# Four early loads on a second queue, and two MoE blocks summed chunk by chunk, in an attention + MoE kernel with a planned order

## The chip, the cores and the metric

The kernel runs on one core of one Trainium2 chip. The metric is the device time of one execution in microseconds (us). Engines are called TensorE (matmuls; PE in the profile), VectorE (DVE), ScalarE (ACT), GpSimd (POOL) and SyncE (SP). SyncE issues the loads and stores; 16 DMA engines move the bytes.

## The reference, cut to what matters

```python
# q, k, v: (4, 8, 768, 64) float32; w_in (512, 2048), w_out (2048, 512) float64
k_sum = k.reshape(B, H, 24, 32, D).max(axis=3)      # block maxima of the keys
v_sum = v.reshape(B, H, 24, 32, D).mean(axis=3)     # block means of the values
scores_l = scale * q @ k.T                          # kept where |i - j| < 16
scores_s = scale * q @ k_sum.T + log(32)
a = softmax(concat([masked scores_l, scores_s]))
x = (a @ concat([v, v_sum])).reshape(3072, 512)     # tokens x (heads * 64)
h = x @ w_in
out = (h - tanh(h)) @ w_out
```

## The kernel before, in words

The 3072 tokens are handled in 8 units of 384 (half a sequence of one batch). Of each unit, attention is computed for four pairs of heads: queries and keys are transposed on TensorE (`prep`), scores are made for three tiles of 128 tokens (`scores`), VectorE and ScalarE do the softmax, the probabilities are transposed, and `values` multiplies them with a value tile `vw`, whose rows hold a window of values and the 24 block means. `x_split` evicts a pair's result (for unit 0 as plain float32 into a tile `xh`, one of four slices per pair). Then the MoE runs in 16 blocks of 128 hidden columns: `moe_in` (four chunks of 128 rows, one per head pair, summed in a PSUM bank `pH`), an activation on ScalarE and VectorE (tiles `gt`, `gu`, `gh`), and `moe_out` into three banks `pY`.

The weights come as float64. 32 loads of 512 KB (weight 2f is block f's part of w_in, weight 2f+1 its part of w_out) go through three places of one buffer, `raw` (weight i uses place i % 3), and `convert` makes float32 of each by bit operations: a scale copy on ScalarE (or VectorE) into `qa` or `tmp`, and on VectorE the low bits (`w low`), the sign (`w sign`; both in place in `raw`) and the join into `wf`. After its first use in unit 0 each weight is split into a high and a low part (`split_whole`) for the later units, which use three faster matmuls instead of one exact one.

The block means of the first batch come from two loads of 768 KB (`first_means(0, g)`, tile `xh`), added pairwise and summed on TensorE with a matrix `blk`; `put_mean` copies them into `vw`.

Nothing is written in the order in which it runs. Every step is a task with a cost per engine; `Plan.schedule` walks through time, and gives the engine that can start first its startable task with the greatest level (the longest path behind it, plus entries of the tables `BIAS` and `KB`; `SL` says when a task may go to a second engine). The resulting order is then emitted, and each engine runs its own instructions strictly in that order, waiting for what they need. In the plan, transfers follow one another on one line, a SyncE task is not started when more than 3 us of transfers (`QUEUE`) or eight loads (`LANES`) are ahead of it, and TensorE's gaps before 100 us (`WARM`) are filled with matmuls of the identity into the bank `pX` (`keep_warm`), whose results nobody uses. The plan has a model of TensorE's clock (`Clock`).

On the chip SyncE's queue issues a load when its buffer is free and the earlier loads have been issued. All instructions are recorded under one line of a helper (L67), so that tiles and not lines tell them apart: `xl` is the first batch's keys, `rawq` queries, `vw` value tiles, `vsum` the value means of the second batch, `chunk` and `vacc` those of the later ones, `k` and `q` the transposed operands, `probw` and `stat` the softmax, `wh` and `wl` the split weights.

Of the kernel before, what the change touches and what calls it, by code (L numbers as in the profile page):

```python
# [12 lines left out]
U32 = mybir.dt.uint32  # L13
# [45 lines left out]
class Engine:  # L59


    def __init__(self, tc, engine):
        self._tc, self._engine = tc, engine

    def __getattr__(self, name):
        op = getattr(self._engine, name)
        return lambda *args, **kwargs: self._tc.keep_in_program_order(op(*args, **kwargs))  # L67


class Task:  # L70
    __slots__ = ("index", "costs", "go", "after", "order", "level", "count", "ready", "next", "start", "engine", "cost", "place", "out", "banks", "behind", "moves", "kind", "name")
# [28 lines left out]
class Plan:  # L100

    SEEN = {PE: 0.2, ACT: 0.16, DVE: 0.13, POOL: 0.1, SP: 0.95}
    ISSUE = 0.5
    QUEUE = 3.0  # L110
    AHEAD = 1.1
    LANES = 8

    def __init__(self):
        self.tasks, self.rings, self.place, self.banks, self.count = [], {}, {}, set(), {}
        self.writer, self.readers, self.touch, self.first = {}, {}, {}, {}

# [7 lines left out]
    def add(self, kind, costs, go, r=(), w=(), before=()):  # L125
        t = Task()
        t.index, t.kind, t.costs, t.go = len(self.tasks), kind, costs, go
# [13 lines left out]
        for base in {key[0] for key in (*r, *w)}:  # L141
# [20 lines left out]
    def schedule(self, idle):  # L162
# [18 lines left out]
        dma, held = 0.0, {DVE: 0.0, POOL: 0.0}  # L181
# [121 lines left out]
def program(  # L303
# [14 lines left out]
    P = 128  # L318
# [831 lines left out]
```

## Time and profile before

| | us |
|---|---|
| median of 3 runs | 740.21 (739.56 to 740.95) |
| the profiled execution | 741.52 |
| its span, first to last instruction | 740.0 |
| TensorE busy | 711.1 (96%) |
| VectorE busy | 508.6 (69%) |
| ScalarE busy | 461.0 (62%) |
| GpSimd busy | 148.0 (20%) |
| mean granted clock of TensorE | 0.988 |
| bytes moved, all by SyncE's queue but for 0.9 MB of instructions | 53.97 MB |

Busy times are sums of records; a busy TensorE is not one at its peak, because matmuls are pipelined. The granted clock is a share of 2.4 GHz; the lower of its two levels, 1.2 GHz, shows as 0.5.

### The profile page before, as it was taken

How to read it: one execution, taken by the hardware profiler on the slowest of the kernel's cores; microseconds unless marked ns; L12 is line 12 of the kernel's file. 1: busy time of each engine (PE TensorE's matmuls, PEld its weight loads, DVE VectorE, ACT ScalarE, POOL GpSimd, SP SyncE). 2: the span in 40 equal slices, each digit the busy share in tenths (PEclk: the TensorE clock that was granted, in tenths of full speed). 3: DMA queues.
4: the chain of work that ended last, by engine and by line, in shares of the span. 5: the costliest groups of instructions: out<-in, count | busy, mean ns of one | idle time of the engine just before them, and what ended most of it. 6: DMA issues, size and time to landing. Idle time of an engine off the chain costs nothing.

```text
span 740.0 us, 13051 instructions
## 1 busy us (share of the span) xinstructions
PE 711.1 (96%) x4205; PEld 589.0 (80%) x4205; DVE 508.6 (69%) x1788; ACT 461.0 (62%) x1388; POOL 148.0 (20%) x229
## 2 busy tenths in 40 slices
PE   7888988999999999999999999999999999999995
PEld 5554444558888888989988889889988899889993
DVE  3789999678876689577765786677665557753332
ACT  2677775557876576667675776766565666754230
POOL 5131000012331013224231133212232132110000
PEclk9899999999999999999999999999999999999998
DMA  9886666602020322422020341212020201101001
GB/s 215 211 221 201 198 200 227 117 2 64 1 63 1 84 85 58 90 51 77 1 63 1 83 108 37 47 35 70 1 62 1 54 30 23 40 2 43 1 0 49
DMA packets 109510, 53.97 MB, mean 73 GB/s; under 512 B 90808, under 2 KB 102776, under 8 KB 109432
## 3 DMA queue, kind: packets, MB, share of 16 engines
q1 hardware_dynamic: 109432, 53.03, 27.5%
q8 instruction: 36, 0.59, 0.3%
q14 instruction: 42, 0.34, 0.2%
HBM read 44.95 MB, written 6.29 MB: 69 GB/s over the span
## 4 chain that ended last, share of the span: by engine, by line
PE 80%; DVE 10%; DMA 3%; SPq 2%; ACT 2%; issue 1%; POOL 1%; DVEq 0%; ACTq 0%
PE pY L67 33%; PE pH L67 33%; PE pS L67 6%; PE pT L67 4%; PE pX L67 3%; DVE raw L67 3%; DVE wf L67 3%; SPq L67 2%; DMA raw<-in_moe_w_in_dram 1%; DVE probw L67 1%; DMA raw<-in_moe_w_out_dram 1%; DMA vw<-in_v_dram 1%; DVE vacc L67 1%; DVE gh L67 0%; DVE stat L67 0%
## 5 line engine op out<-in xcount | busy, mean ns | idle before, releaser
L67 PE MATMUL pH<-xh,wf 128*128 128x384 f32 x548 | 188.0, 377 | 5.0 <-ACT gt L67 3.2
L67 PE MATMUL pY<-wf,gh 128*128 128x512 f32 x432 | 177.8, 438 | 0.5 <-DVE gh L67 0.5
L67 ACT ACTIVATE gu<-pH 128x384 f32<-128x384 f32 x128 | 62.6, 489 | 131.7 <-PE pH L67 124.5
L67 PEld LDWEIGHTS pH<-xh,wf 128*128 128x128 f32 x548 | 103.2, 190 | 26.9 <-ACT gt L67 4.4
L67 POOL TENSOR_TENSOR gl<-gv,gh 128x384 fp32r<-128x384 f32 x57 | 58.5, 1027 | 243.6 <-ACT gh L67 117.2
L67 PEld LDWEIGHTS pY<-wf,gh 128*128 128x128 f32 x432 | 80.6, 190 | 22.3 <-issue 11.2
L67 DVE CUSTOM_DVE_ANT_0 prob<-pS,mask 64x118 f32<-64x118 f32 x288 | 80.2, 278 | 24.6 <-PE pT L67 9.1
L67 PE MATMUL pH<-xh,wh 128*128 128x384 f32 x252 | 88.2, 350 | 0.0
L67 PE MATMUL pH<-xl,wh 128*128 128x384 f32 x252 | 85.0, 337 | 0.0
L67 ACT ACTIVATE prob<-prob,stat 128x118 f32<-128x118 f32 x175 | 67.8, 392 | 26.6 <-DVE stat L67 22.4
L67 PE MATMUL pY<-wh,gh 128*128 128x512 f32 x168 | 70.9, 422 | 0.0
L67 ACT ACTIVATE gu<-gu 128x384 f32<-128x384 f32 x128 | 66.8, 523 | 0.0
L67 PE MATMUL pY<-wh,gl 128*128 128x512 f32 x168 | 66.3, 394 | 0.0
L67 DVE CAST gh<-gv 128x384 fp32r<-128x384 f32 x59 | 21.2, 359 | 59.9 <-PE pY L67 59.6
L67 ACT ACTIVATE gt<-pH 128x384 f32<-128x384 f32 x128 | 61.7, 482 | 0.0
L67 DVE TENSOR_TENSOR gv<-gu,gt 128x384 f32<-128x384 f32 x68 | 38.9, 572 | 20.5 <-ACT gu L67 13.4
L67 POOL TENSOR_TENSOR gv<-gu,gt 128x384 f32<-128x384 f32 x44 | 45.3, 1029 | 34.6 <-DVE gl L67 16.1
L67 PEld LDWEIGHTS pH<-xh,wh 128*128 128x128 f32 x252 | 47.4, 188 | 2.2 <-issue 0.5
L67 PE MATMUL pS<-k,q 128*128 128x364 f32 (+1 forms) x176 | 44.9, 336 | 3.3 <-DVE stat L67 2.7
L67 PEld LDWEIGHTS pH<-xl,wh 128*128 128x128 f32 x252 | 47.3, 188 | 0.0
L67 ACT ACTIVATE probT<-pT 118x256 f32<-118x256 f32 x86 | 32.6, 379 | 20.9 <-PE pT L67 20.8
L67 PEld LDWEIGHTS pS<-k,q 128*128 128x128 f32 x176 | 30.7, 190 | 13.1 <-issue 5.1
(185 smaller groups left out, 1484.1 us busy)
## 6 DMA issues: line engine op xcount, KB each, us to landing
raw<-in_moe_w_in_dram SPq DMA_DIRECT2D x16, 512.0 KB
raw<-in_moe_w_out_dram SPq DMA_DIRECT2D x16, 512.0 KB
rawq<-in_q_dram SPq DMA_DIRECT2D x48, 128.0 KB
out_dram<-tmp SPq DMA_DIRECT2D x23, 256.0 KB
raw<-in_k_dram SPq DMA_DIRECT2D x24, 192.0 KB
vw<-in_v_dram SPq DMA_DIRECT2D x40, 96.0 KB
vw<-in_v_dram SPq DMA_DIRECT2D x48, 64.0 KB
chunk<-in_v_dram SPq DMA_DIRECT2D x16, 192.0 KB
```

The costliest lines, as they stand in the source:

```text
L67: return lambda *args, **kwargs: self._tc.keep_in_program_order(op(*args, **kwargs))
```

## The change

- `convert`: the loads of weights 0 and 2 are issued by ScalarE instead of SyncE. `first_means(0, g)`: so are the two 768 KB loads of the first batch. All other loads stay with SyncE. In the plan such a load takes 0.5 us (`ISSUE`) of ScalarE's time and its bytes join the one line of transfers; it is not held back by `QUEUE` or `LANES`.
- `Plan.schedule`: before 60 us, a SyncE load whose transfer is costed at over 1.25 us and that follows a smaller one is planned to hold the line for 0.9 us more.
- `moe_in`: in unit 0, blocks 0 and 1 become four tasks each, one per chunk, of 0.68 us, instead of one of 2.65. The matmuls are the same ones.
- The tables: `BIAS` 763 entries instead of 539 (360 as before), `SL` 44 instead of 43 (7 as before), `KB` 158 instead of 156 (44 as before).

```diff
...
+    LARGE, TURN = 1.25, 0.9
...
             t.start, t.engine, t.cost = now, e, t.costs[e]
+            if t.moved is not None:
+
+                t.moves = max(dma, now + self.AHEAD)
+                dma = t.moves + t.moved
...
             if e == SP:
                 free[e] = now + self.ISSUE
                 t.moves = max(dma, now + self.AHEAD)
-                dma = t.moves + t.cost
+                dma = t.moves + t.cost + (self.TURN if t.cost > self.LARGE and not large and now < 60.0 else 0.0)
+                large = t.cost > self.LARGE
                 landed.append(dma + self.SEEN[e])
                 release(t, dma + self.SEEN[e])
             else:
                 free[e] = clock.run(now, t.cost) if e == PE else now + t.cost
-                release(t, free[e] + self.SEEN[e])
+                release(t, free[e] + self.SEEN[e] if t.moved is None else dma + self.SEEN[SP])
...
-    def dma(kind, go, nbytes, run, r=(), w=(), before=()):
+    def dma(kind, go, nbytes, run, r=(), w=(), before=(), by=SP):
         rate = 227e3 if run < 512 else 302e3 if run < 1024 else 356e3 if run < 4096 else 390e3
-        do(kind, SP, nbytes / rate, go, r, w, before)
+        if by is not SP:
+            plan.add(kind, {by: plan.ISSUE}, lambda: go(engines[by]), r, w, before, nbytes / rate)
+            return
+        do(kind, SP, nbytes / rate, lambda: go(sync), r, w, before)
...
-        dma("w load", load, P * 8 * DM, 1024 if i % 2 == 0 else 4096, w=RAW)
+        dma("w load", load, P * 8 * DM, 1024 if i % 2 == 0 else 4096, w=RAW, by=ACT if i in (0, 2) else SP)
...
-        dma("v load", lambda: sync.dma_start(at(base), v[b, HG * g:HG * (g + 1)].rearrange("h (r t) d -> r h (t d)", t=6)), S * HG * D * 4, 1536, w=[(base, 0)])
+        dma("v load", lambda e: e.dma_start(at(base), v[b, HG * g:HG * (g + 1)].rearrange("h (r t) d -> r h (t d)", t=6)), S * HG * D * 4, 1536, w=[(base, 0)], by=SP if b else ACT)
...
         if u == 0:
-            def go():
+            def go(cs):
+                for c in cs:
+                    tensor.matmul(at(ph)[:, :U], at(("wf", i))[:, P * c:P * (c + 1)], at(xf)[:, c], start=c == 0, stop=c == NC - 1)
+            if f < 2:
+
                 for c in range(NC):
-                    tensor.matmul(at(ph)[:, :U], at(("wf", i))[:, P * c:P * (c + 1)], at(xf)[:, c], start=c == 0, stop=c == NC - 1)
-            do("in", PE, 2.65, go, r=[(("wf", i), 0)] + [(xf, c) for c in range(NC)], w=[(ph, 0)])
+                    do("in" if c == NC - 1 else "in part", PE, 0.68, lambda c=c: go([c]), r=[(("wf", i), 0), (xf, c)], w=[(ph, 0)])
+            else:
+                do("in", PE, 2.65, lambda: go(range(NC)), r=[(("wf", i), 0)] + [(xf, c) for c in range(NC)], w=[(ph, 0)])
             split_whole(i)
             return
```

## Rows read from the trace of the kernel before

**Rows 1.** Busy us (instructions) of each engine by stretches; then clock, DMA share, GB/s.
```profile
0.00:12.00 12.00, 7.99 (x46) 6.93 (x47) 1.30 (x7) 1.99 (x3) 8.31 (x34) 1.00 0.82 194
12.00:26.00 14.00, 11.11 (x62) 7.13 (x60) 12.59 (x55) 9.54 (x38) 3.84 (x10) 1.00 1.09 241
26.00:33.00 7.00, 6.31 (x32) 4.81 (x32) 3.61 (x17) 1.95 (x5) 0.21 (x1) 0.54 0.61 148
33.00:50.00 17.00, 13.99 (x135) 9.36 (x134) 15.59 (x58) 14.98 (x50) 4.85 (x12) 0.99 0.88 230
...
60.00:128.00 68.00, 61.87 (x242) 33.34 (x242) 66.36 (x174) 48.18 (x129) 4.35 (x8) 1.00 0.64 206
...
140.00:731.00 591.00, 589.89 (x3636) 517.52 (x3634) 393.87 (x1444) 370.85 (x1132) 124.33 (x163) 1.00 0.17 41
...
sum 740.00, PE 711.06 PEld 588.95 DVE 508.58 ACT 460.96 POOL 148.01; mean PE 79.01 PEld 65.44 DVE 56.51 ACT 51.22 POOL 16.45
```

**Rows 2.** Timeline, VectorE and ScalarE: start, us, what, [idle before <-releaser].
```profile
8.66 0.96 DVE L67 TENSOR_TENSOR xh<-xh 128x768 f32<-128x768 f32 x1 [7.33 <-DMA xh<-in_v_dram]
...
11.19 0.37 ACT L67 ACTIVATE mean<-pT 24x256 f32<-24x256 f32 x1 [9.11 <-PE pT L67]
```

**Rows 3.** Timeline, TensorE, near 26 us.
```profile
26.66 1.41 PE L67 MATMUL pX<-probT,vw 118*64 118x64 f32 x16 [2.34 <-DMA vw<-in_v_dram]
```

**Rows 4.** Chain of waits from 60 to 145 us, shares by line.
```profile
by line: DVE raw L67 24.1%; DVE wf L67 20.0%; DMA raw<-in_moe_w_in_dram 11.9%; PE pH L67 8.4%; DVE probw L67 6.7%; PE pY L67 6.3%; issue 5.1%; DVE vacc L67 4.0%; PE pT L67 3.6%; DVE gh L67 3.0%; DVE stat L67 1.0%; DVE tmp L67 0.9%; PE pX L6
```

**Rows 5.** SyncE's waits from 0 to 140 us: total us, times, longest.
```profile
SPq L67 <- DVE wf L67: 27.2, 15, 3.7
```

**Rows 6.** Timeline of SyncE's queue: the four loads, and weight 3.
```profile
1.88 0.54 SPq L67 DMA_DIRECT2D xh<-in_v_dram  x1
...
10.28 0.78 SPq L67 DMA_DIRECT2D xh<-in_v_dram  x1
...
17.16 0.43 SPq L67 DMA_DIRECT2D raw<-in_moe_w_in_dram  x1
...
19.22 0.43 SPq L67 DMA_DIRECT2D raw<-in_moe_w_in_dram  x1
...
45.06 0.35 SPq L67 DMA_DIRECT2D raw<-in_moe_w_out_dram  x1
```

**Rows 7.** Groups of conversion instructions, 0 to 140 us: busy us, mean ns.
```profile
L67 DVE TENSOR_SCALAR raw<-raw 128x512 uint16<-128x512 uint16 x32 | 23.2, 746 | 0.1
...
L67 DVE SCALAR_TENSOR_TENSOR wf<-tmp,raw 128x512 uint32<-128x512 uint32 x21 | 14.4, 692 | 0.1
L67 DVE TENSOR_SCALAR raw<-raw 128x512 uint32<-128x512 uint32 x32 | 13.5, 426 | 3.4 <-DMA raw<-in_moe_w_out_dram 2.8 <-DMA raw<-in_moe_w_in_dram 0.6
...
L67 ACT ACTIVATE tmp<-raw 128x512 f32<-128x512 f32 x16 | 10.6, 677 | 7.9 <-DMA raw<-in_moe_w_in_dram 6.4 <-DMA raw<-in_moe_w_out_dram 1.0
```

**Rows 8.** Timeline, VectorE and ScalarE, 36 to 53 us: evictions of pairs, conversion.
```profile
36.22 0.48 ACT L67 ACTIVATE xh<-pX 128x384 f32<-128x384 f32 x1
...
36.95 0.75 DVE L67 TENSOR_SCALAR raw<-raw 128x512 uint32<-128x512 uint32 x2
...
43.88 0.47 ACT L67 ACTIVATE xh<-pX 128x384 f32<-128x384 f32 x1
...
44.27 0.72 DVE L67 SCALAR_TENSOR_TENSOR wf<-qa,raw 128x512 uint32<-128x512 uint32 x1
...
46.03 0.69 DVE L67 SCALAR_TENSOR_TENSOR wf<-tmp,raw 128x512 uint32<-128x512 uint32 x1
...
52.55 0.43 DVE L67 TENSOR_SCALAR raw<-raw 128x512 uint32<-128x512 uint32 x1 [2.63 <-DMA raw<-in_moe_w_out_dram]
```

**Rows 9.** Timeline, TensorE: first query transposes; warm-up and first MoE blocks.
```profile
11.08 0.55 PE L67 MATMUL pH<-ident,rawq 128*128 128x128 f32 x3
...
49.24 0.49 PE L67 MATMUL pX<-ident 128*128 128x128 f32 x2
49.56 5.33 PE L67 MATMUL pH<-xh,wf 128*128 128x384 f32 x16
```

More of the change, by code (lines that the diff above doesn't have):

```diff
@@ new lines @@
+SL = {('w scale', 0, 'vector'): 1, ('k again', 2, 'gpsimd'): 0.6, ('normal', 0, 'scalar'): 0.6, ('q high', 2, 'vector'): -0.6, ('top low', 1, 'gpsimd'): 1, ('normal', 2, 'scalar'): 1, ('k again', 2, 'scalar'): 1.5, ('k high', 0, 'vector'): 0.6, ('top low', 2, 'gpsimd'): -0.6, ('p out', 0, 'vector'): 1, ('g high', 2, 'vector'): 0.6, ('w scale', 1, 'vector'): 4, ('sum guard', 2, 'gpsimd'): 0.3, ('p out', 1, 'vector'): -0.6, ('g high', 1, 'vector'): -0.3, ('x whole', 2, 'vector'): -0.6, ('x high', 2, 'vector'): -0.3, ('k again', 1, 'gpsimd'): 0.6, ('w high part 2', 0, 'vector'): 0, ('top put', 2, 'vector'): 0, ('q again', 2, 'scalar'): 0, ('q again', 1, 'gpsimd'): 0.6, ('top put', 0, 'vector'): 4, ('k again', 1, 'scalar'): 2.5, ('top put', 2, 'scalar'): 0.3, ('p out', 2, 'vector'): 1.5, ('normal', 1, 'scalar'): -0.6, ('top high', 1, 'scalar'): -0.3, ('g', 2, 'vector'): 1.5, ('top put', 1, 'scalar'): 2.5, ('k high', 2, 'vector'): 2.5, ('x high', 0, 'vector'): -0.6, ('x high', 1, 'vector'): 0.6, ('q again', 2, 'gpsimd'): -0.3, ('sum guard', 1, 'gpsimd'): 4, ('pair', 2, 'vector'): 0, ('q again', 1, 'scalar'): 1, ('top put', 1, 'vector'): 2.5, ('q high', 1, 'vector'): 0.6, ('q high', 0, 'vector'): 0.6, ('k high', 1, 'vector'): -0.6, ('g low', 1, 'vector'): 2.5, ('w high part 2', 1, 'vector'): 0.3, ('top high', 2, 'scalar'): -0.6}
@@ new lines @@
+KB = {('square', 1): 220, ('exp', 2): 102, ('out', 2): -19, ('values', 1): 28, ('w scale', 1): 112, ('k turn', 2): -38, ('g high', 2): -96, ('k low', 1): -494, ('g high', 1): -340, ('top put', 2): 151, ('pick', 2): 18, ('w low part', 1): 63, ('series', 2): 64, ('top put', 0): 109, ('square', 2): 57, ('mean turn', 1): -73, ('w low', 1): -57, ('w load', 1): -48, ('w low', 0): 97, ('x high', 0): 38, ('exp', 0): 28, ('series', 1): 130, ('p turn', 2): -50, ('inverse', 2): 137, ('x high', 2): 37, ('values', 2): 2, ('w high part', 1): 19, ('out', 1): -11, ('q low', 1): -459, ('big', 1): -123, ('tanh', 1): -169, ('direct', 1): 24, ('scores', 2): 6, ('in', 2): -93, ('normal', 2): -41, ('mean out', 0): -57, ('min', 2): -53, ('mean out', 1): 102, ('cube', 2): -140, ('exp', 1): -111, ('mean turn', 0): 122, ('in', 0): -13, ('q high', 0): 6, ('top max', 0): -64, ('top low', 0): -194, ('g low', 2): 18, ('k high', 1): -58, ('k turn', 0): 23, ('w shift', 0): -153, ('top turn', 0): 15, ('p out', 2): 11, ('sum out', 0): -33, ('k high', 0): 16, ('min', 0): 42, ('big', 2): 18, ('sum guard', 0): 7, ('sum', 0): 28, ('w load', 0): 56, ('q turn', 0): 56, ('values', 0): 30, ('w high part', 0): 111, ('k load', 0): 191, ('v load', 0): -38, ('p out', 0): 11, ('min', 1): 82, ('normal', 0): 75, ('sum guard', 1): -293, ('x high', 1): 186, ('q high', 1): -43, ('inverse', 1): -61, ('g low', 1): 12, ('p turn', 0): 18, ('k turn', 1): 37, ('top pre', 0): 17, ('square', 0): 82, ('pick', 1): -55, ('p out', 1): 61, ('in', 1): 21, ('p turn', 1): -31, ('pick', 0): 21, ('direct', 0): -139, ('cube', 0): 30, ('w sign', 1): -216, ('g', 1): -48, ('cube', 1): -7, ('big', 0): 97, ('w sign 2', 0): 34, ('q turn', 1): 21, ('normal', 1): -28, ('w sign 2', 1): 17, ('q again', 1): -53, ('mean put', 1): 101, ('w high part 2', 1): -123, ('g', 0): 84, ('g', 2): 15, ('x low', 0): -1, ('seen max', 2): 2000, ('w shift', 1): -15, ('y store', 2): 148, ('chunk load', 0): 8, ('top put', 1): -188, ('k high', 2): -195, ('k again', 2): -113, ('tanh', 0): -67, ('top turn', 2): -3, ('x low', 1): -89, ('w sign', 0): 90, ('w scale', 0): -57, ('chunk load', 2): 3, ('x whole', 2): -89, ('w high part 2', 0): 272, ('w low part 2', 2): 70, ('top high', 2): 21, ('chunk sum', 2): 79, ('k load', 1): 7, ('mean turn', 2): -121, ('w high part 2', 2): 144, ('k low', 2): 125, ('k again', 1): -307, ('top low', 1): -114, ('top low', 2): -166, ('mean put', 0): 21, ('out', 0): -61, ('q load', 2): -92, ('inverse', 0): 9, ('top high', 1): -20, ('tanh', 2): 61, ('seen', 2): 2000, ('series', 0): -26, ('k load', 2): 92, ('q high', 2): -100, ('scores', 1): 24, ('q again', 2): 9, ('pad', 2): -162, ('w low part 2', 1): 115, ('const', 0): -168, ('chunk sum', 0): -2, ('q load', 1): -74, ('x low', 2): 12, ('q load', 0): -2, ('v load', 1): 20, ('mean put', 2): 43, ('top max', 1): -65, ('seen turn', 2): 2000, ('w sign', 2): -130, ('top turn', 1): 15, ('mean out', 2): -226, ('mean copy', 0): 145, ('y out', 2): 61, ('w join', 2): 107, ('sum guard', 2): -22, ('w join', 0): -32, ('q low', 2): -78, ('q turn', 2): 8, ('w join', 1): -71, ('v load', 2): -87, ('pair', 2): 30, ('in part', 2): -11}
@@ L70 @@
 class Task:
-    __slots__ = ("index", "costs", "go", "after", "order", "level", "count", "ready", "next", "start", "engine", "cost", "place", "out", "banks", "behind", "moves", "kind", "name")
+    __slots__ = ("index", "costs", "go", "after", "order", "level", "count", "ready", "next", "start", "engine", "cost", "place", "out", "banks", "behind", "moves", "moved", "kind", "name")
 HELD = {"pair", "mean copy", "w join", "w shift", "w low", "w sign", "w low part", "w low part 2", "w low part 3", "w high part", "w high part 2", "w scale", "normal", "g high", "g low", "g", "cube", "big", "k again", "q again", "top pre", "sum guard"}
@@ L123, in users, with add @@
         return {t for key in keys for t in (self.writer[key], *self.readers.get(key, ()))}
-    def add(self, kind, costs, go, r=(), w=(), before=()):
+    def add(self, kind, costs, go, r=(), w=(), before=(), moved=None):
         t = Task()
+        t.moved = moved
         t.index, t.kind, t.costs, t.go = len(self.tasks), kind, costs, go
@@ L180, in schedule @@
         landed = [0.0] * self.LANES
-        dma, held = 0.0, {DVE: 0.0, POOL: 0.0}
+        dma, large, held = 0.0, False, {DVE: 0.0, POOL: 0.0}
         clock = Clock()
@@ L599, in load_k @@
         for h in range(HG):
-            dma("k load", lambda h=h: sync.dma_start(tile()[:, :, h], k[b, HG * g + h].rearrange("(c r) d -> r c d", c=6)), S * D * 4, D * 4, w=[keys[h]], before=before)
+            dma("k load", lambda e, h=h: e.dma_start(tile()[:, :, h], k[b, HG * g + h].rearrange("(c r) d -> r c d", c=6)), S * D * 4, D * 4, w=[keys[h]], before=before)
     def first_means(b, g, tag):
@@ L625, in sum_chunks @@
             dr = v[b, HG * g:HG * (g + 1)].rearrange("h (n t) d -> (h n) t d", t=32)
-            dma("chunk load", lambda st=st, dr=dr, c=c: sync.dma_start(at(st)[:96], dr[:, 8 * c:8 * c + 8, :]), 96 * 2048, 2048, w=[(st, 0)])
+            dma("chunk load", lambda e, st=st, dr=dr, c=c: e.dma_start(at(st)[:96], dr[:, 8 * c:8 * c + 8, :]), 96 * 2048, 2048, w=[(st, 0)])
             def total(c=c, st=st):
@@ L647, in load_q @@
         for i in range(NT):
-            dma("q load", lambda i=i: sync.dma_start(at(rawq)[:, i], qd[b, t0 + P * i:t0 + P * (i + 1), HG * g:HG * (g + 1), :]), P * HG * D * 4, D * 4, w=[(rawq, i)])
+            dma("q load", lambda e, i=i: e.dma_start(at(rawq)[:, i], qd[b, t0 + P * i:t0 + P * (i + 1), HG * g:HG * (g + 1), :]), P * HG * D * 4, D * 4, w=[(rawq, i)])
     def load_v(u, g):
@@ L656, in rows @@
             s0 = t0 + off + P * i
-            dma("v load", lambda: sync.dma_start(at(vw)[r0:r1, i, half], vd[b, s0:s0 + r1 - r0, hs, :]), (r1 - r0) * HG * D * 4, D * 4, w=[vw_keys(vw, i, half)[m] for m in parts])
+            dma("v load", lambda e: e.dma_start(at(vw)[r0:r1, i, half], vd[b, s0:s0 + r1 - r0, hs, :]), (r1 - r0) * HG * D * 4, D * 4, w=[vw_keys(vw, i, half)[m] for m in parts])
         for i in range(NT):
             if u % 2 == 0 and i == 0:
-                dma("v load", lambda: sync.dma_start(at(vw)[0:WIN + 1, 0, 0], vd[b, 0:1, hs, :].broadcast_to([WIN + 1, HG, D])), (WIN + 1) * HG * D * 4, D * 4, w=[vw_keys(vw, 0, 0)[0]])
+                dma("v load", lambda e: e.dma_start(at(vw)[0:WIN + 1, 0, 0], vd[b, 0:1, hs, :].broadcast_to([WIN + 1, HG, D])), (WIN + 1) * HG * D * 4, D * 4, w=[vw_keys(vw, 0, 0)[0]])
                 rows(0, [0], WIN + 1, 64, WIN + 1, 0)
@@ L684, in put_mean @@
             else:
-                dma("mean put", lambda to=to, x=x: sync.dma_start(to(), x), NT * NB * HG * D * 4, 1024, r=[MEAN[g]], w=keys)
+                dma("mean put", lambda e, to=to, x=x: e.dma_start(to(), x), NT * NB * HG * D * 4, 1024, r=[MEAN[g]], w=keys)
     def operands(u, p):
@@ L1018, in store_y @@
         r = u * U + P * i
-        dma("y store", lambda: sync.dma_start(out[r:r + P, :], at(ys)), P * DM * 4, 2048, r=[(ys, 0)])
+        dma("y store", lambda e: e.dma_start(out[r:r + P, :], at(ys)), P * DM * 4, 2048, r=[(ys, 0)])
     NS = NP * SLOTS * NU
```

10 lines of the change are left out of this document (4 added, 6 removed).

## The prediction

> **What bounds the kernel now.** I read three views: the busy time by stretches of the span, then the chain of waits in the stretch that is not full of matmuls, then SyncE's own waits. In the first the reader is to see where TensorE is not busy: over the whole span it is busy for 711.06 of 740 us, and from 140 to 731 us for 589.89 of 591, at full clock [rows 1]. I take that part, and the last 9 us (last tile out, last check), as fixed. What can move lies in the first 140 us, in three regimes:
> - 0 to 26 us: the transfers. The DMA share is 0.82 and then 1.09 (records overlap, so over 1 is possible), and VectorE is idle for 10.7 of the first 12 us, 7.33 of them in one wait for the first value tile [rows 1, 2].
> - 26 to 60 us: mixed. From 26 to 33 us TensorE has a granted clock of 0.54, which is mostly its lower level, 1.2 GHz, after it had stood idle for 2.34 us until a value tile landed [rows 1, 3].
> - 60 to 128 us: VectorE, busy 66.36 of 68 us, while TensorE has 6.1 us idle. The chain of waits of this stretch runs mostly through VectorE's work on the weights (raw 24.1%, wf 20.0%) [rows 1, 4]. SyncE's waits say the same from the other side: in the first 140 us its queue waited 27.2 us for VectorE to be done with a weight, so that a raw place could be filled again [rows 5].
>
> So the end moves by as much as VectorE's conversion work can be brought out of the stretch 12 to 128 us into the time before it, and by what TensorE loses to idle time and to the low clock in 12 to 60 us.
>
> **The sum's base.** The profiled execution took 741.52 us: 740.0 us of span and 1.5 us around it. That is 1.3 us above the median of the runs, 740.21. I work out a difference from the trace and take it off both.
>
> **1. Four loads leave SyncE's queue for ScalarE's.** They are the two 768 KB value loads and the 512 KB w_in loads of MoE blocks 0 and 1 (weights 0 and 2). In the trace they were issued at 1.88, 10.28, 17.16 and 19.22 us and held SyncE's queue for 0.54 + 0.78 + 0.43 + 0.43 = 2.18 us [rows 6]. On ScalarE each costs an issue of the same kind, 0.4 to 0.8 us. None of the four waits for a buffer: both value tiles and raw places 0 and 2 are unused then. The plan offers a task to its engine as soon as its inputs are there, and ScalarE had nothing but a table load before 11.19 us, 9.11 us of it in one wait [rows 2]. So I expect all four at the front of ScalarE's queue, issued by about 4 us, and their cost there at nothing. If instead the plan leaves the two weights where they were, 0.86 us of issue falls among the exponentials of 16 to 20 us, where ScalarE is nearly full; the bounds of the issue are 0 and +2.2 us.
>
> The bytes do not move faster by it: the transfers were the full resource already. What changes is their order. The weights 0 and 2 come some 10 us sooner, and 1.3 MB of keys and queries share the engines with them.
>
> **The gain: conversion in VectorE's idle start.** A weight costs VectorE 0.426 (low bits) + 0.746 (sign) + 0.692 (join) = 1.86 us, by the means of 32, 32 and 21 such instructions [rows 7]. For weights 0 and 2 that is 3.73 us. In the trace it ran from 36.95 us (low bits of both) to 46.7 (joins at 44.27 and 46.03), amid a VectorE that is 92% busy from 33 to 50 us [rows 1, 8]. If the two weights land by 8 to 12 us, these 3.73 us go into the 10.7 idle ones [rows 1]. ScalarE's two scale copies (0.68 us each [rows 7]) go with them into its idle start. Everything VectorE does later then has 3.73 us less before it.
>
> The bounds: 0, if the weights land only after 12 us, when VectorE is busy 12.59 of 14 us [rows 1] and they merely displace attention work; and above 3.73, because the join also frees a raw place. The load of weight 3 was issued at 45.06 us, right behind the join of weight 0, and landed at 52.5 us; VectorE stood idle for it for 2.63 us, and it had 3.4 us idle from 26 to 33 us [rows 1, 6, 8]. With the place free at some 12 us those loads come sooner and could fill both: 3.73 + 2.63 + 3.39 = 9.8 us is the far end. I take 3.7: the two weights are certain to want the idle time, while the later loads have to find room on transfer engines that are 0.88 busy from 33 to 50 us [rows 1].
>
> **2. The first two MoE blocks, chunk by chunk.** The two blocks' 16 matmuls ran together, in 5.33 us from 49.56 us on, when all four head pairs were done [rows 9]. Now three quarters of them, 12/16 x 5.33 = 4.0 us of TensorE, can run as soon as the tiles of pairs 0 to 2 are there (three evictions, the first at 36.22, the last at 43.88 us [rows 8]) and the weight is joined. TensorE has 3.0 us idle from 33 to 50 us, and two pairs of warm-up matmuls of 0.49 us that such work would replace, one of them at 49.24 us [rows 1, 9], so the 4.0 us fit. The two PSUM banks are not in the way: what last used them before is the fourth pair's preparation, well ahead of pair 2's eviction. What is late next is not TensorE: behind it VectorE waited for weight 3 until 52.55 us [rows 8] and was then nearly full. So by itself this is worth between 0 and 2.6 us (that wait), and I take 0. What it does is keep TensorE from being the one that holds back the 3.7 us of part 1. The cost of three more waits per block is hidden in that same idle time.
>
> **3. The plan's model and the tables.** The plan now adds 0.9 us to a large transfer that follows a small one, before 60 us, and more than half of the table entries differ. That changes only the order on the engines. From 140 us on there is no more than 1.1 us of idle time to win. The order from 12 to 128 us can go either way. One effect has a row: warm-up matmuls are put in where the plan itself sees TensorE wait. In this trace none was put into the wait that ends at 26.66 us, and TensorE then ran 6.31 us of work at 0.54 of its clock: 6.31 x 0.46 = 2.9 us lost [rows 1, 3]. A plan that has the value tiles land later would fill that wait. Bounds: -2.9 us, and +2.9 if another such wait opens elsewhere. I take 0.
>
> **The sum:** -3.7 us. Profiled 741.5 - 3.7 = 737.8; median 740.2 - 3.7 = 736.5 us.
>
> **A rule that speaks against it.** From 12 to 26 us the transfer engines' share is 1.09 at 241 GB/s [rows 1]. The Trainium skill (DMA: Bandwidth & Descriptors, section Issuing engines are not separate DMA queues) says that loads issued from several engines run on the same 16 transfer engines and that only the issuing time is saved. By that rule alone the change would be worth at most the 2.18 us of SyncE's queue, and nothing where the engines are full. The trace agrees as to the full engines; the gain that I count is one of order, which the rule leaves open.
>
> **Rivals.**
> - **Both pay (faster than forecast).** The 3.7 us, and the wait up to 26.66 us covered so that the clock stays up: -3.7 - 2.9 = -6.6, 733.6 us. For it: in the plan's new model large transfers end later, so it sees such waits [rows 3]. Against: it needs the order to come out so.
> - **Nothing (same).** The transfers from 2 to 26 us are the same bytes at the same rate; value tiles land at 26.6 us as before, the weights land after 12 us, and VectorE converts them in the same crowded stretch: 0, 740.2 us, within 1.5.
> - **Keys and queries late (slower).** The four loads are 2560 KB (2.62 MB) with runs of 1024 and 1536 bytes; keys and queries have runs of 256. If the large ones are served ahead, the first pair's two key and three query loads (0.79 MB) land when 3.41 MB have moved: at 241 GB/s 14.1 us, from 2 us on, so at 16.1 us instead of 11.08, when the first query transposes ran [rows 1, 9]. VectorE's queue is in order, so a conversion planned early and landing late also stands in front of the keys' copies. The late start is covered by the 2.34 us that TensorE waited anyway before 26.66 us [rows 3]; beyond that it costs: 5.0 - 2.3 = +2.7, 742.9 us, and +5.0 (745.2) without the cover. It decides when the first query transpose runs after 13.4 us. Against it: VectorE's early idle time is won all the same if the conversions come before.
>
> **Chances.** Forecast 0.40 (735 to 738.7), both pay 0.22 (down to 731 with the freed raw place), nothing 0.17, slower 0.21. A difference under 0.2% (1.5 us) can't be told from none here. So faster 0.62, same 0.17, slower 0.21. The range of 8 in 10 goes from 731.0 (most of the far end, -9.2 us) to 743.5 (the slower rival with a little more); the forecast's own range is 735.0 to 738.7.
>
> **What would show it.** Right: four loads early in ScalarE's queue; low-bits and sign instructions on raw before 13 us on VectorE; the load of weight 3 issued well before 45 us; pH from xh matmuls in groups of two before 49 us; VectorE's full stretch ending near 124 us instead of 128. Wrong: weights 0 and 2 landing after 13 us, or a VectorE wait for them with key copies behind it; the first query transposes after 13.4 us; a stretch of granted clock near 0.5 longer than that of 26 to 33 us; or any idle time of TensorE between 140 and 731 us beyond the 1.1 us of now.

## The result, and the profile after

The changed kernel takes 732.25 us (median of 4 runs) against 740.58 us for the kernel before in the same measurement: ratio 0.9898, 95% interval 0.9875 to 0.9921, that is 8.3 us less by the medians and 7.6 by the ratio. The profiled execution takes 733.46 us, with a span of 731.7. The forecast was 736.5 us, range 731.0 to 743.5. The direction is right and the time lies in the range, but the gain is twice the -3.7 us of the sum, and the time is outside the forecast's own range; the nearest case is the rival "both pay", 733.6 us.

The stretches of the changed kernel, with the columns of [rows 1]:

```profile
0.00:12.00 12.00, 7.71 (x38) 5.62 (x38) 2.50 (x9) 1.89 (x3) 7.58 (x34) 1.00 0.92 250
12.00:26.00 14.00, 12.04 (x85) 9.90 (x85) 11.75 (x41) 8.06 (x26) 1.16 (x4) 1.00 1.02 188
26.00:33.00 7.00, 6.80 (x59) 4.89 (x58) 6.56 (x31) 5.93 (x23) 0.48 (x2) 1.00 0.77 197
33.00:50.00 17.00, 15.69 (x124) 9.81 (x123) 16.31 (x67) 14.95 (x48) 4.06 (x7) 1.00 0.87 231
50.00:60.00 10.00, 9.25 (x37) 5.08 (x36) 9.82 (x21) 8.92 (x25) 2.08 (x2) 1.00 0.87 252
60.00:128.00 68.00, 64.05 (x233) 33.68 (x233) 66.16 (x175) 49.21 (x126) 2.44 (x4) 1.00 0.66 203
128.00:140.00 12.00, 12.00 (x67) 6.97 (x61) 5.07 (x16) 5.79 (x18) 0.00 (x0) 1.00 0.82 170
140.00:722.00 582.00, 579.59 (x3602) 511.12 (x3602) 334.15 (x1305) 368.06 (x1137) 249.38 (x289) 1.00 0.16 41
...
sum 731.70, PE 709.76 PEld 588.88 DVE 452.31 ACT 464.61 POOL 267.17; mean PE 78.86 PEld 65.43 DVE 50.26 ACT 51.62 POOL 29.69
```

Two rows of before that were not shown, for the same comparison:

```profile
50.00:60.00 10.00, 8.11 (x26) 4.02 (x24) 7.25 (x16) 6.79 (x18) 2.11 (x2) 1.00 0.81 210
...
128.00:140.00 12.00, 11.77 (x34) 5.84 (x35) 8.01 (x23) 6.09 (x18) 0.00 (x0) 0.86 0.91 179
```

The reader is to see four things. The gain was made before 140 us: there the new kernel has 591.7 us left to run, the old one 600.0, and behind that point TensorE is full in both (589.89 of 591 us, 579.59 of 582). VectorE's early stretch hardly filled up (2.50 us busy of the first 12, from 1.30), but the holes behind it did: 6.56 of 7 us from 26 to 33 us (from 3.61), 9.82 of 10 from 50 to 60 us (from 7.25). The granted clock is 1.00 in every stretch up to 722 us, where it was 0.54 from 26 to 33 us and 0.86 from 128 to 140. And the new order gives GpSimd some of VectorE's work behind 140 us (VectorE 393.87 to 334.15 us, GpSimd 124.33 to 249.38), with TensorE as full as before.

In TensorE's account the 8.3 us are: idle time 28.9 to 21.9 us (-7.0); low clock, 2.9 us (6.31 x 0.46) and 1.6 us (11.77 x 0.14), gone (-4.5); warm-up matmuls, 7.9 to 11.5 us of records (+3.6); the rest -0.4.

Conversion itself is further ahead. VectorE's joins into `wf`, one for each weight that is converted, number 6 up to 60 us before (first two lines) and 8 after, and its work on `raw` is 10.32 us before and 15.99 after:

```profile
L67 DVE SCALAR_TENSOR_TENSOR wf<-tmp,raw x4: 681/689/715, 46.0 to 59.3; 128x512 uint32<-128x512 uint32 x4
L67 DVE SCALAR_TENSOR_TENSOR wf<-qa,raw x2: 670/698/725, 44.3 to 54.9; 128x512 uint32<-128x512 uint32 x2
...
L67 DVE SCALAR_TENSOR_TENSOR wf<-tmp,raw x5: 684/693/1685, 39.0 to 59.1; 128x512 uint32<-128x512 uint32 x5
L67 DVE SCALAR_TENSOR_TENSOR wf<-qa,raw x3: 680/681/693, 13.1 to 57.7; 128x512 uint32<-128x512 uint32 x3
```

The early queue entries and conversions. ScalarE's and SyncE's queues, VectorE and TensorE of the changed kernel (start, us, what), four answers, and behind ScalarE's queue two pieces of the chain of waits:

```profile
0.80 1.14 ACTq L67 DMA_DIRECT2D xh<-in_v_dram  x2
1.97 6.31 ACTq L67 DMA_DIRECT2D raw<-in_moe_w_in_dram  x2
8.31 1.28 ACT L67 ACT_TABLE_LOAD   x1 [8.31 <-DMA xl<-in_k_dram]
9.60 0.37 ACT L67 ACTIVATE mean<-pT 24x256 f32<-24x256 f32 x1
```

```profile
1.31 6.58 DMA xl<-in_k_dram
7.91 7.24 DMA raw<-in_moe_w_in_dram
```

```profile
32.02 0.38 SPq L67 DMA_DIRECT2D raw<-in_moe_w_out_dram  x1
```

```profile
11.76 1.21 DVE L67 TENSOR_SCALAR raw<-raw 128x512 uint32<-128x512 uint32 x2 [1.20 <-DMA raw<-in_moe_w_in_dram]
13.08 0.69 DVE L67 SCALAR_TENSOR_TENSOR wf<-qa,raw 128x512 uint32<-128x512 uint32 x1
15.17 1.21 DVE L67 TENSOR_SCALAR raw<-raw 128x512 uint32<-128x512 uint32 x2 [1.40 <-DMA raw<-in_moe_w_in_dram]
...
31.17 0.54 DVE L67 COPY xh<-pX 128x384 f32<-128x384 f32 x1
```

```profile
14.36 0.49 PE L67 MATMUL pH<-ident,rawq 128*128 128x128 f32 x3
...
22.03 2.40 PE L67 MATMUL pX<-ident 128*128 128x128 f32 x20
...
28.75 0.45 PE L67 MATMUL pX<-probT,vw 118*64 118x64 f32 x8
...
35.44 0.91 PE L67 MATMUL pH<-xh,wf 128*128 128x384 f32 x2
```

The four loads are at the head of ScalarE's queue. The row of 6.31 us is two issues with a wait between them: 0.56 us at 1.97 and 0.37 us at 7.91. By the chain of waits the fourth load stood until a load of keys had landed at 7.89 us, and the table load and the first eviction (9.60 us, for matmuls that ended at 8.72) stood behind it. The weights land at 11.7 and 15.1 us, the first query transposes run 3.3 us later than before [rows 9]; the value products run at 28.75 us without a wait, behind score tiles that stood behind them before; weight 3 is loaded from 32.02 us instead of 45.06 [rows 6]; the first pair's result is evicted at 31.17 us instead of 36.22 [rows 8]; the first MoE part runs at 35.44 us.

### The profile page after: what moved, and what is told of

It reads as the page before. It is cut to its first block, busy times and chain, and to the rows that moved or that the text cites. A ratio compares the mean times of both kernels' runs of the same rounds, so it can differ in the third digit from the quotient of the medians.

```text
span 731.7 us, 13092 instructions
## 1 busy us (share of the span) xinstructions
PE 709.8 (97%) x4237; PEld 588.9 (80%) x4237; DVE 452.3 (62%) x1661; ACT 464.6 (63%) x1402; POOL 267.2 (37%) x342
## 4 chain that ended last, share of the span: by engine, by line
PE 81%; DVE 10%; DMA 4%; ACT 2%; issue 1%; SPq 0%; DVEq 0%; ACTq 0%
PE pY L67 35%; PE pH L67 33%; PE pS L67 6%; PE pT L67 5%; PE pX L67 3%; DVE wf L67 3%; DVE raw L67 2%; DMA raw<-in_moe_w_in_dram 2%; DVE probw L67 1%; DMA xl<-in_k_dram 1%; DVE vacc L67 1%; DVE prob L67 1%; DMA raw<-in_moe_w_out_dram 1%; ACT probw L67 1%; DVE stat L67 0%
## 5 line engine op out<-in xcount | busy, mean ns | idle before, releaser
L67 POOL TENSOR_TENSOR gl<-gv,gh 128x384 fp32r<-128x384 f32 x112 | 114.4, 1021 | 214.8 <-ACT gh L67 162.6
L67 POOL TENSOR_TENSOR gv<-gu,gt 128x384 f32<-128x384 f32 x112 | 114.1, 1019 | 48.3 <-ACT gu L67 32.6
L67 ACT ACTIVATE prob<-prob,stat 128x118 f32<-128x118 f32 x164 | 63.7, 393 | 31.8 <-DVE stat L67 27.1
L67 ACT ACTIVATE gh<-gv 128x384 fp32r<-128x384 f32 x94 | 49.1, 522 | 40.2 <-PE pY L67 39.5
L67 DVE TENSOR_SCALAR prob<-prob,stat 128x118 f32<-128x118 f32 x124 | 42.4, 374 | 2.3
L67 DVE CAST gh<-gv 128x384 fp32r<-128x384 f32 x18 | 6.7, 373 | 53.1 <-PE pY L67 52.6
```

## The experiments

Times are medians beside runs of the kernel before on the same chip; what is compared is the ratio, with its interval. Ten kernels move, drop or re-issue the instructions that are named and keep every other one in the order that the plan gave (the emitted list is edited); two are planned anew. A trace shows one execution, which can lie some 2 us off the median (738.23 for 740.15 us in the run with the old tables). The first five edit the kernel before, the next five the changed one.

**Warm-ups ahead of the value products (before).**

```diff
+        x = where("values", 0)
+        todo[x:x] = [d] * 10        # d: a keep_warm task
```

> The kernel before, with ten warm-up matmuls of the identity (2.4 us) put into TensorE's queue just ahead of the value products that waited until 26.66 us; nothing else moves. Theory A (the low clock after that wait is a good part of the 8.3 us): the granted clock from 26 to 33 us rises from 0.54 to near 1.0 and the time falls by up to 2.9 us, to about 737.7. Rival B (that stretch is set by the value tiles and by VectorE, not by TensorE's speed): the clock rises and the time stays within 1 us of 740.6.

Measured: 740.22 us, ratio 0.9981 (0.9962 to 1.0000): 1.4 us less, by the interval anything from nothing to 2.8, so the time alone decides little between the two theories. Two stretches of this kernel, and TensorE, GpSimd and VectorE in the second of them:

```profile
26.00:33.00 7.00, 6.68 (x61) 5.10 (x59) 5.46 (x24) 4.39 (x16) 0.51 (x3) 1.00 0.59 121
33.00:50.00 17.00, 12.25 (x105) 9.07 (x105) 12.01 (x50) 12.31 (x42) 4.23 (x12) 0.80 0.76 208
```

```profile
44.18 1.10 PE L67 MATMUL pY<-ident,probw 128*118 128x128 f32 x4 [3.94 <-DVE probw L67]
```

```profile
41.23 1.80 POOL L67 TENSOR_TENSOR vsum<-vsum 128x768 f32<-128x768 f32 x1 [4.92 <-DMA vsum<-in_v_dram]
43.12 0.51 POOL L67 TENSOR_SCALAR stat<-stat 128x2 f32<-128x2 f32 x2
```

```profile
43.36 0.17 DVE L67 RECIPROCAL stat<-stat 128x2 f32<-128x2 f32 x1 [4.52 <-POOL stat L67]
```

The clock is up from 26 to 33 us, as meant, and much of the gain is given back ten microseconds later. GpSimd's queue holds the pairwise sum of a value-mean load (`vsum`) that has not landed; behind it stand two small additions of the softmax, VectorE's reciprocal waits 4.52 us for them, TensorE 3.94 us for VectorE, and the clock falls there instead (0.80). In the trace of before that pairwise sum waited 0.59 us and began at 38.52 us; here GpSimd is there 1.6 us earlier and the load lands 2.7 us later. Why it lands later is not shown.

**Value products later (before).**

```diff
+        late = [todo.pop(where("values", n)) for n in (0, 1)]
+        x = where("k turn", 3) + 1
+        todo[x:x] = late
```

> The kernel before, with the first two value products moved back in TensorE's queue, behind two score tiles, four transposes of probabilities and the fourth pair's key transposes that stood behind them; nothing else moves. Theory A (the wait of 2.34 us with the low clock after it is what the changed kernel lost): the idle time before 26.66 us and the low clock both go, -2.3 - 2.9 = -5.2 us, about 735.4. Rival B: what is moved ahead of the value products waits in its turn, or the tiles landing at 26.5 us set the rest of the stretch: within 1 us of 740.6.

Measured: 741.73 us, ratio 1.0008 (0.9988 to 1.0027): nothing. The same place takes it back:

```profile
39.59 1.80 POOL L67 TENSOR_TENSOR vsum<-vsum 128x768 f32<-128x768 f32 x1 [4.65 <-DMA vsum<-in_v_dram]
```

**The four loads first, by ScalarE (before).**

```diff
+        early = [todo.pop(where(*n)) for n in (("v load", 0), ("v load", 11), ("w load", 0), ("w load", 2))]
+        todo[:0] = early            # and issued by scalar instead of sync
```

> The kernel before, with the four loads issued first thing by ScalarE, and every other instruction in the order of before (the conversions too, late). By the prediction this brings nothing by itself, since VectorE still converts at 37 us: 0, or up to +2.7 us (743.3) if keys and queries land late by more than the 2.3 us of cover. By the rule of the Trainium skill (DMA: Bandwidth & Descriptors, Issuing engines are not separate DMA queues) only issue time is saved: between 0 and -2.2 us, 738.4 to 740.6.

Measured: 740.15 us, ratio 0.9988 (0.9972 to 1.0004): no difference, as both the prediction and the rule allow. The low clock has moved: it is 1.00 from 26 to 33 us, and 0.76 from 12 to 26 us, behind 2.6 us in which TensorE waits for queries:

```profile
12.00:26.00 14.00, 12.95 (x59) 9.39 (x60) 9.08 (x35) 6.86 (x23) 3.18 (x7) 0.76 1.02 193
```

**The loads and the early conversion (before).** As above, and:

```diff
+        work = [todo.pop(where(*n)) for n in (("w scale", 0), ("w low", 0), ("w sign", 0), ("w join", 0), ("w low", 2), ("w sign", 2))]
+        x = where("mean out", 0) + 1
+        todo[x:x] = work
```

> As the run with the loads first in ScalarE's queue, and the conversion that the changed kernel has early is moved up as well: all of weight 0, low bits and sign of weight 2, right behind the first evicted value means. This is the prediction's main term alone. The prediction: VectorE's 0.43 + 0.75 + 0.69 + 0.43 + 0.75 = 3.0 us leave the crowded stretch, about 737.6. Rival (the weights land after 12 us and displace the attention's work on VectorE): 740.6 to 743.5, with the first query transposes after 13.4 us.

Measured: 740.81 us, ratio 1.0006 (0.9986 to 1.0026): nothing, not the 3.0 us. VectorE, and SyncE's queue, in this kernel:

```profile
16.23 0.66 DVE L67 TENSOR_REDUCE th<-pH 128x16 f32<-128x512 f32 x1
...
53.46 0.43 DVE L67 TENSOR_SCALAR raw<-raw 128x512 uint32<-128x512 uint32 x1 [1.97 <-DMA raw<-in_moe_w_out_dram]
```

```profile
45.01 0.37 SPq L67 DMA_DIRECT2D raw<-in_moe_w_out_dram  x1
```

Weight 3's raw place is free by 14 us, but its load still stands at 45.01 us in SyncE's queue, behind other loads, and VectorE still waits for it, at 53.46 instead of 52.55 us [rows 8]. What was won at 37 us was lost at the start: VectorE's first key maxima ran at 16.23 us, behind the conversion, instead of 12.10, TensorE waited 2.90 us for them, and its clock from 12 to 26 us was 0.88. Up to 60 us this kernel has 5 weights converted, one fewer than the kernel before.

**The same, with weight 3's load behind weight 1's (before).**

```diff
+        third = todo.pop(where("w load", 3))
+        x = where("w load", 1) + 1
+        todo[x:x] = [third]
```

> The kernel before with the four loads first in ScalarE's queue, the early conversion, and besides the load of weight 3 moved up in SyncE's queue from 45 us to right behind that of weight 1 (about 31 us), since its raw place is free by 14 us. With the loads and the conversion alone VectorE still stood idle for 1.97 us at 53.46 us, waiting for weight 3, and nothing was won. If that queue position is what ate the gain: the wait goes, and with it up to 2.0 us, about 738.8. If not, because the fourth pair's result at 51.5 us sets the rest: within 1 us of 740.8.

Measured: 739.46 us, ratio 0.9979 (0.9964 to 0.9994), 1.6 us less. So the queue position was a part of it (2.0 us against the run without it, give or take 1.9 by the two intervals); VectorE's waits that are left there are now 1.05 us for another load of `moe_w_out`, at 54.04 us, and 2.01 us for GpSimd behind `vsum`, at 42.91 us.

**One queue (changed kernel).**

```diff
-            plan.add(kind, {by: plan.ISSUE}, lambda: go(engines[by]), r, w, before, nbytes / rate)
+            plan.add(kind, {by: plan.ISSUE}, lambda: go(sync if small_only else engines[by]), r, w, before, nbytes / rate)
```

> The changed kernel with its order as it is, but the four loads issued by SyncE, at the head of its queue, where the plan has them. If only the order of the loads and of the work matters: within 1.5 us of 732.3 (at most the 2.2 us of issue more). If the second queue itself matters, because keys and queries get their share of the transfer engines beside the large loads: with one queue they wait for 2.62 MB, some 9 to 11 us, and the time rises by 3 us or more, to over 735.

Measured: 733.17 us, ratio 0.9899 (0.9881 to 0.9917), the same as the changed kernel's 0.9898. SyncE's queue of this kernel:

```profile
1.31 1.08 SPq L67 DMA_DIRECT2D xh<-in_v_dram  x2
...
2.98 2.72 SPq L67 DMA_DIRECT2D raw<-in_moe_w_in_dram  x2
5.74 3.54 SPq L67 DMA_DIRECT2D rawq<-in_q_dram  x3
```

No worth of the second queue shows (the two intervals leave room for some 2 us); the order carries the gain.

**Blocks whole (changed kernel).** Blocks 0 and 1 run whole at the place of their last part.

```diff
-... lambda c=c: go([c]), ...
+... lambda c=c: go(range(NC)) if c == NC - 1 else None, ...
```

> The changed kernel with its order as it is, but the matmuls of MoE blocks 0 and 1 all run where the last of their four parts stands. The prediction gave the parts nothing by themselves, since VectorE is full behind them: within 1.5 us of 732.3. Rival: the 4.0 us of TensorE work that the parts put into gaps before 50 us come back in full behind the fourth pair, and the activation behind them too: up to +4 us, 736.3.

Measured: 735.45 us, ratio 0.9919 (0.9899 to 0.9938), 1.6 us slower than the changed kernel by the two ratios, whose intervals overlap, and 2.3 us slower than the runs beside it with one queue (733.17) and with fewer warm-ups (733.20). Its stretch shows where it comes from:

```profile
33.00:50.00 17.00, 12.90 (x110) 8.80 (x109) 15.39 (x66) 14.21 (x46) 4.05 (x7) 0.84 0.81 221
```

TensorE is busy 2.8 us less in the stretch, and its clock falls (0.84 for 1.00).

**Fewer warm-ups from 22 to 24.4 us (changed kernel).**

```diff
+        todo = [t for t in todo if hasattr(t, "costs") or not 20.0 < t.start < 27.0]
```

> The changed kernel with its order as it is, less the ten warm-up matmuls (2.4 us) from 22 to 24.4 us. Clock theory: TensorE idles there, the granted clock falls toward 0.5 for some us behind it and the time rises by 2 to 3 us, to 734.5 to 735. Rival (the stretch is set by VectorE and ScalarE): within 1 us of 732.3.

Measured: 733.20 us, ratio 0.9891 (0.9873 to 0.9909): the same as with all of them. The edit goes by planned times, and took out seven of the ten, not all: of the 20 records (2.40 us) that stood at 22.03 us 6 are left. TensorE idles, but the clock stays up:

```profile
22.49 0.83 PE L67 MATMUL pX<-ident 128*128 128x128 f32 x6
24.89 0.65 PE L67 MATMUL pY<-ident,probw 128*118 128x128 f32 x4 [1.57 <-DVE probw L67]
```

```profile
24.00:26.00 2.00, 1.11 (x7) 0.82 (x8) 1.92 (x10) 1.32 (x6) 0.57 (x2) 1.00 0.47 106
26.00:28.00 2.00, 1.89 (x14) 1.37 (x12) 1.84 (x9) 0.97 (x4) 0.00 (x0) 1.00 0.74 164
```

The changed kernel has 36 other such records between 8 and 17 us, against 8 in the kernel before, and the runs with the early loads had a clock of 0.76 and 0.88 from 12 to 26 us without them. No run takes these 36 out.

**Conversion back to 28 us (changed kernel).**

```diff
+        work = [todo.pop(where(*n)) for n in (("w scale", 0), ("w low", 0), ("w sign", 0), ("w join", 0), ("w high part 2", 0), ("w low part 2", 0), ("w low", 2), ("w sign", 2))]
+        x = where("w load", 3)
+        todo[x:x] = work
```

> The changed kernel with its order as it is, but the early conversion (all of weight 0 and its split, low bits and sign of weight 2; 3.7 us of VectorE) moved from 12 to 16 us back to about 28 us, just ahead of the load of weight 3. This undoes the prediction's main term inside the changed kernel. The prediction: +3 to +3.7 us, 735.5 to 736. Rival (the order of the rest makes the gain; the early conversion was won in one place and paid for by late keys in another, as on the kernel before): within 1.5 us of 732.5.

Measured: 737.24 us, ratio 0.9953 (0.9939 to 0.9968): 4.1 us slower than the changed kernel. VectorE and two stretches of this kernel:

```profile
32.06 1.19 DVE L67 TENSOR_SCALAR raw<-raw 128x512 uint32<-128x512 uint32 x2
```

```profile
12.00:26.00 14.00, 12.95 (x89) 10.03 (x88) 8.12 (x34) 6.86 (x24) 1.17 (x4) 1.00 0.99 188
...
33.00:50.00 17.00, 12.54 (x87) 7.36 (x85) 15.27 (x63) 11.44 (x39) 3.95 (x7) 0.90 0.61 173
```

VectorE has 3.6 us less to do from 12 to 26 us (8.12 for 11.75), does it at 32 to 37 us instead, and TensorE waits 2.9 us for the softmax behind it. In this order the early conversion is worth 4.1 us, give or take 2.0 by the two intervals. That is not the prediction's term alone: the split of weight 0 goes with it, the join of weight 2 does not, and the load of weight 3 is late with it (34.08 us for 32.02). Up to 60 us 6 weights are converted, as in the kernel before.

**Key maxima first (changed kernel).**

```diff
+        work = [todo.pop(where(*n)) for n in (("w low", 2), ("w sign", 2), ("w low part 2", 0))]
+        x = where("mean copy", 0) + 1
+        todo[x:x] = work
```

> The changed kernel, with VectorE's key maxima and two copies of the means moved ahead of the low bits and sign of weight 2 and the split of weight 0, for which VectorE waited 1.40 us until 15.17 us while the transposed keys lay ready from 15.1 us; the chain of waits runs through that place. If the chain's start counts: -1 to -1.6 us, about 731. If what follows absorbs it, as on the kernel before: within 1 us of 732.5.

Measured: 733.70 us, ratio 0.9900 (0.9877 to 0.9924): absorbed.

**Code and tables apart, planned anew.** The changed code with the three tables of before:

> The changed kernel's code (loads by ScalarE, blocks in parts, large transfers planned longer) with the three tables of before, planned anew. If the code's three edits make the gain: 732 to 735. If the order that the new tables choose makes it: 738 to 743, that is nothing or a loss.

Measured: 740.15 us, ratio 0.9985 (0.9968 to 1.0002). The code of before with the new tables:

> The code of before with the three new tables, planned anew. If the tables alone make the gain: 732 to 735. If they only fit the changed code: 738 to 745. If both this and the run with the old tables stay near 740, the gain is of the two together.

Measured: 746.25 us, ratio 1.0075 (1.0048 to 1.0102), 5.6 us slower than before. Stretches 60 to 128 us of the first and 33 to 50 us of the second:

```profile
60.00:128.00 68.00, 61.64 (x240) 32.63 (x239) 66.22 (x165) 46.09 (x118) 3.94 (x5) 1.00 0.71 210
```

```profile
33.00:50.00 17.00, 9.75 (x88) 6.70 (x87) 12.84 (x48) 9.33 (x31) 2.97 (x5) 0.85 0.76 207
```

The changed code with old tables has the early conversion, the holes before 60 us filled nearly as well, and a clock of 1.00, and still gains at most 2.4 us by its interval. It has 6 weights converted by 60 us, not 8, and VectorE's 66.2 us of the next stretch serve TensorE less (61.64 us busy for 64.05). The new tables on the old plan leave TensorE idle for 7 of 17 us. Neither half makes the gain; the two together do.

## Why the prediction was right in direction, and short in size

- **The bound** held. Everything moved before 140 us, VectorE fills 66 of 68 us from 60 to 128 us in both kernels, and the end moved with the conversion brought ahead. The two weights more by 60 us are the prediction's two, 3.73 us of VectorE. Over all fourteen kernels the four with 8 weights by 60 us take 732.25 to 733.70 us, the ten with 5 or 6 take 735.45 to 746.25. That is a reading of traces, and no test that holds the rest fixed.
- **The main term**, conversion in early idle time, held in the changed kernel's order: 3.7 us forecast, 4.1 us by undoing nearly the same work. Its place was off: the fourth load was issued at 7.91 us, not by 4, the weights landed at 11.7 and 15.1 us, not by 8 to 12, and the work went into waits from 11.8 to 16.9 us that the late keys and queries opened, not into the first 12 us. Added alone to the kernel before it is worth nothing. So it is not a term that could be added to any order.
- **The step that failed** is "I take 3.7", with the two holes, 2.63 and 3.39 us, at nothing. Those are the holes that filled: 2.95 us more of VectorE from 26 to 33 us and 2.57 us more from 50 to 60 us. The sum's own far end, 9.8 us, stood nearer to the truth than its value, partly by luck: loads of weights, which were to fill the first hole, did not. From 26 to 33 us the changed kernel converts nothing, and in the kernel before VectorE stood there waiting for TensorE at its low clock:

```profile
29.66 0.07 DVE L67 MEMSET pY<- 64x15 f32 x1 [1.35 <-PE pY L67]
...
31.69 0.35 DVE L67 CUSTOM_DVE_ANT_0 probw<-pY,wide 128x182 f32<-128x182 f32 x1 [1.96 <-PE pY L67]
```

  So this hole and the low clock are one loss, and closed together. In the second hole 1.5 of the 2.57 us are two copies beside GpSimd that took 2.91 us at 52.53, for 0.68 each elsewhere. The freed raw place did bring weight 3's load forward by 13 us; on the kernel before that had to be done by hand to be worth 1.6 us.
- **The low clock**, 2.9 us, was also taken at nothing, and went. The rival that counted it came nearest, but its reason, warm-ups in the wait, is not borne out: with seven of the ten taken out the time is the same. The value products stand behind more work, and TensorE has no wait over 0.28 us from 20 to 33 us (1.57 with the seven out). What the earlier warm-ups do is untested.
- **The parts of blocks 0 and 1**, taken at 0 with an end of 2.6 us, are worth some 1.6 to 2.3 us.
- **The rule on issuing engines** (the Trainium skill, "DMA: Bandwidth & Descriptors", section "Issuing engines are not separate DMA queues"), that they bring no transfer capacity: the trace agrees. From 0 to 26 us 219 GB/s were moved before and 217 after, and with one queue the time is the same. A gain was left open as one of order, and it was one of order.
- **The slower rival's test** failed as a test. The first query transposes ran at 14.36 us, past the 13.4 at which I said it would decide, weight 2 landed past 13 us with key copies behind VectorE's wait for it, and the kernel is faster. It is 3.3 us late at the query transposes, 2.1 at the value products, and 5.0 us ahead when the first pair is evicted, with TensorE at its full clock between the last two.

Why a correct term was worth nothing alone is read from the traces of the first five runs: between 33 and 54 us the old order has three waits close behind one another (GpSimd's queue behind `vsum`, weight 3's place in SyncE's queue, the fourth pair), and time won ahead of one is spent at the next. Only the place of weight 3 was tested by an edit. In the changed kernel no small softmax addition stands on GpSimd from 33 to 54 us, but no run took these additions off GpSimd in the kernel before. What each single table entry contributes was not separated, and so the share of the gain beyond the 4.1 us has no single cause that a run shows. From 60 to 140 us VectorE has less left to convert (40.65 us on `raw` for 47.16); that this is why its time serves TensorE better there is likely, and not tested.

## What to carry to other kernels

Where several in-order queues wait on each other, price an edit together with the next wait behind its stretch, and look in each queue for a small instruction that stands behind a big one waiting for a load. Here a saving found in idle time was worth its size only in an order planned around it: undoing it in the final kernel cost 4.1 us, adding it to the first one brought nothing. Do both, since the first can flatter an edit and the second can hide it. The second issuing queue brought no bandwidth here (219 and 217 GB/s); the same order on one queue was as fast. And check what an edit did in its trace: one that goes by planned times can miss some of its instructions.

## What the runs showed of the hardware

- A load that waited held its engine's queue. Issuing a load took ScalarE 0.37 to 0.63 us, within the 0.4 to 0.8 that I had priced, nearly as on SyncE [rows 6]. But the fourth stood from 2.53 to 7.91 us until a load of keys had landed, and ScalarE's table load ran behind it at 8.31 us and its first eviction 0.9 us late. I had looked only for waits for a buffer.
- Beside GpSimd's sum of two value-mean halves (1.81 us) single instructions of VectorE took much longer. In the kernel before the 128x182 one below took 1.86 us, for 0.31 at 35.18; in the changed kernel a join of 0.69 us took 1.69 at 41.55. No run separates the cause.

```profile
38.52 1.81 POOL L67 TENSOR_TENSOR vsum<-vsum 128x768 f32<-128x768 f32 x1 [0.59 <-DMA vsum<-in_v_dram]
38.59 1.86 DVE L67 TENSOR_SCALAR probw<-probw,stat 128x182 f32<-128x182 f32 x1
```

- An idle time of TensorE of 1.57 us, at 23.3 to 24.9 us, in a stretch that kept it 1.11 of 2 us busy, left the granted clock at 1.00; 2.34 us before 26.66 us, with 0.32 of 2 us busy from 24 to 26 us, was followed by 0.50 from 28 to 32 us. The first is of the run with fewer warm-ups, the second of the kernel before:

```profile
24.00:26.00 2.00, 0.32 (x2) 0.00 (x0) 1.75 (x10) 2.00 (x11) 0.67 (x3) 1.00 0.90 130
...
28.00:30.00 2.00, 2.00 (x6) 1.19 (x5) 0.38 (x2) 0.00 (x0) 0.00 (x0) 0.50 0.61 139
```
